# Pooled attention, then a gated MLP: joining a pair's two sums on one set of partitions, a first load on another queue, and a new order

## The chip, the cores and the metric

The kernel runs on one core of a Trainium2 chip. The metric is the device time of one execution in microseconds. The profile is one execution recorded by the hardware profiler; its span is the time from the first to the last instruction, and the execution's own time is a little longer. PE is TensorE, PEld its weight loads, DVE VectorE, ACT ScalarE, POOL GpSimd, SP SyncE, whose queue issues nearly all DMAs; SPq is that issuing.

## The reference

```python
def _attn_ref(q, k, v):                       # q, k, v: (4, 8, 1152, 64) float32
    q_pool = q.reshape(B, H, S // 2, 2, D).mean(axis=3)
    scores = scale * np.matmul(q_pool, k.transpose(0, 1, 3, 2))
    scores = scores - np.max(scores, axis=-1, keepdims=True)
    attn = np.exp(scores)
    attn = attn / (np.sum(attn, axis=-1, keepdims=True) + 1e-09)
    return np.matmul(attn, v)

def _moe_ref(x, w_in, w_out):                 # w_in: (512, 2048), w_out: (2048, 512), float64
    h = x @ w_in
    g = h * np.clip(h + 3.0, 0.0, 6.0) / 6.0
    return g @ w_out

x = attn_out.transpose(0, 2, 1, 3).reshape(B * S // 2, H * D)     # (2304, 512)
return _moe_ref(x, w_in, w_out)
```

## The kernel before

The attention runs over 16 pairs g of heads (4 batches, 4 pairs of two heads j), each with 576 pooled queries in two halves h of 288 (HQ); a unit is one pair and one half. Keys are 9 tiles t of 128. For each unit, scores with the keys on the partitions go to PSUM (line 406 in the first four pairs, the early ones, with plain float32 matmuls for both heads in one tile; line 410 in the late pairs, with operands split into a high and a low part); ScalarE copies them to the tile `s` (step "cp") and VectorE keeps a running maximum (step "mx", line 428). `fold`, `best` and `spread` (steps "s1" to "s3") turn the maxima, reduce them and spread them back over the partitions; `lessen` (step "su", line 449) subtracts, `expo` exponentiates on ScalarE, `values` multiplies with v (line 474).

The denominators come in three ways. In the early pairs `sums_of_four` (line 499) adds up on TensorE, and `pick_sums` (line 510) turns the sums so that queries are on the partitions. In the late pairs GpSimd adds the nine exponentiated tiles of one head to one (`total`, line 467, four steps "ad"). In pairs 4 to 9 `sums` (line 491) multiplies those tiles by a column of ones, six matmuls for a unit; VectorE takes the reciprocal of the small result (`recip`), `widen` repeats it 64 times, `quotient` (line 546) turns it back and `divide` multiplies. From pair 10 on (`BROAD`) `wide_sums` (line 524) multiplies them by 64 columns of ones, so that a sum stands on each of 64 partitions; `take_sums` adds the epsilon on ScalarE, `invert` takes three reciprocals of 128 x 96 on VectorE (line 532), `times` multiplies. `split_x` splits the result in two parts, and `spill` writes both to DRAM.

The MLP weights are float64 and are converted on the chip: `load_raw` loads half a block (lines 572 and 577, one buffer for each half), `convert` takes seven steps "cv" over ScalarE, GpSimd and VectorE (lines 592 to 616; steps 2 to 4 hold a PSUM slot), and `save_w` writes the result to DRAM. There are 16 blocks f of two halves. The first ten (FCV) use one of the three PSUM slots "v", which the early scores use too. When they and the early maxima are done, the step "second" closes these pools and opens those of the late pairs and of the MLP.

Six chunks of 256 tokens of the MLP run mixed with the late pairs: `do_layer` (line 187), relu, gate, split, `do_project` (line 220), 16 steps each. The last 768 tokens come after the attention in a loop of their own, whose last results `store` scales and `write` writes in pieces of at most 96 rows.

The order is made by a planner at build time (class `Order`). Each step has a place, a cost for each engine on which it may run (a third number is added to its place for that engine), the steps that it needs, and the rooms that it takes and frees. Whenever an engine is free, the ready step with the lowest place goes next; if nothing of a lower place is ready, a later one does. The result is each engine's order, which holds on the chip. The constants at the top (FIRST, STEPS, LAG for the MLP, CONV and CSTEP for the conversion, PER for a pair, AT for the parts of a pair) make the places. `load_k`, `load_q`, `load_v` and all other loads are issued by SP in this order.

Of the kernel before, what the change touches and what calls it, by code (L numbers as in the profile page):

```python
# [11 lines left out]
F32 = mybir.dt.float32  # L12
# [9 lines left out]
FIRST, STEPS, LAG = 91.73, (6.01, 2.86), 10.18  # L22
CONV, CSTEP = 9.8, 8.97
# [3 lines left out]
OFF = ((1, 2), (2,))  # L27
BROAD = 10
ADDS = (2, 4, 0)
CUT = 200  # L30
PER, AT, NGL = 25.1, (-3.2, 3.43, -1.21, 3.22, 4.48, 22.08, 16.57), 10.01
TAIL = 768


def adds(g, h):
    return ADDS[0] if g < ADDS[2] else ADDS[1]


# [92 lines left out]
def pooled_attention_then_gated_mlp(ctx, tc, q, k, v, w_in, w_out, out):  # L131
# [96 lines left out]
    def write(ob, c0):  # L228
        r = 0
        while r < P:  # L230
            blk, p0 = divmod(c0 + r, QP)
            n = min(QP - p0, P - r)
            b, tt = divmod(blk, QT)
            nc.sync.dma_start(out=ov[b, tt, p0:p0 + n, :], in_=ob[r:r + n, :])
            r += n

    def store(pool, po, c0):
        for t, o in enumerate(po):
            ob = pool.tile([P, DM], F32, tag="ob", name="ob", bufs=len(po))
            scale(ob, o, "DVE" if t % 2 else "ACT")  # L240
            write(ob, c0 + t * P)
# [18 lines left out]
    with ExitStack() as a:  # L260
# [14 lines left out]
        ones = const.tile([P, D], F32, name="ones")  # L275
        nc.vector.memset(ones, 1.0)
        pick = const.tile([P, 2], F32, name="pick")
# [3 lines left out]
        eps = const.tile([P, 1], F32, name="eps")  # L281
        nc.vector.memset(eps, EPS)
# [146 lines left out]

        def fold(eng, u):  # L430
# [89 lines left out]

        def wide_sums(eng, g, h):
            ps = d_t["p", g, h] = ps_m["s"].tile([P, HQ], F32, tag="s", name="psr")
            for j in range(2):
                nc.tensor.matmul(ps[j * D:(j + 1) * D, :], ones, d_t.pop((g, h, j))[:, 0], start=True, stop=True)  # L524

        def take_sums(eng, g, h):
            x_t[g, h] = xo.tile([P, HQ], F32, tag="x", name="x")
            nc.scalar.activation(out=x_t[g, h], in_=d_t.pop(("p", g, h)), func=AF.Identity, bias=eps)

        def invert(eng, g, h, n):  # L530
            x = x_t[g, h][:, n * QP:(n + 1) * QP]
            nc.vector.reciprocal(out=x, in_=x)

        def times(eng, g, h):
            x = x_t[g, h]
            nc.vector.tensor_tensor(out=x, in0=av_t.pop((g, h)), in1=x, op=ALU.mult)
# [129 lines left out]
        room = dict(kr=1, qr=1, qp=1, vr=2, kT=2, v=3, q=2, mb=2, s=3, S=SBUFS, m=2, st=1, d=2, av=1, x=2, xo=2,  # L666
# [4 lines left out]
        UNIT = PER / 4  # L671

        for g in range(NG):
            lead = PER * (g - 1)
            early = g == 0
            add(("lk", g), lead - 8, {"SP": (940, 3500, 1800)}, partial(load_k, g=g), (), ("kr",))
            add(("lq", g), lead - 7, {"SP": (470, 2500, 1800)}, partial(load_q, g=g), (), ("qr",))
            z = lead + AT[0]
# [223 lines left out]
```

## Time and profile before

| | us |
|---|---|
| median of 3 runs (lowest, highest) | 921.22 (919.14, 922.02) |
| the profiled execution | 917.72 |
| its span, first to last instruction | 915.9 |
| TensorE busy in the span | 871.7 |
| mean granted TensorE clock, share of full speed | 0.983 |

A row of a group of instructions names the line, the engine and operation, the tile written and the tile read, the shapes and the count; then busy time, mean duration of one in ns, and idle time of the engine ahead of them with what ended it. One float32 matmul may show as several records. Busy time is the union of the records, whose ends are modelled for TensorE.

### The profile page before, as it was taken

To read this page: it belongs to the slowest core of one execution; us is meant where nothing else is said; L and a number is where in the kernel's file an instruction comes from. 1 tells how busy PE (TensorE), PEld (TensorE's weight loads), DVE (VectorE), ACT (ScalarE), POOL (GpSimd) and SP (SyncE) were. 2 spreads that over 40 slices of the span, in tenths; PEclk is the share of its full clock that TensorE was granted. 3 is DMA by queue.
4 is the path that set the end of the run, shared out by engine and by line. 5 is a ranking of instruction groups with operands and counts; after the bars stand their busy time and mean duration, and the time that the engine had idled before them with its cause. 6 is when DMAs were issued, how large, how long until landed. Compare 5 with 4: busy or idle time off the path is not lost.

```text
span 915.9 us, 16896 instructions
## 1 busy us (share of the span) xinstructions
PE 871.7 (95%) x5988; PEld 683.8 (75%) x5988; DVE 639.2 (70%) x1196; ACT 585.3 (64%) x1239; POOL 527.4 (58%) x460
## 2 busy tenths in 40 slices
PE   5689997899999999999999999999999999999997
PEld 3344544467787788888988788888888877888886
DVE  2887888887978888867877777777868754322222
ACT  3677978767877767767777676776757753322222
POOL 1666887476977866768667584848576666000000
PEclk9798999899999999999999999999999999999999
DMA  8688665689976485888757787897857749533323
GB/s 218 199 270 261 209 226 200 201 269 355 300 248 186 152 247 184 255 256 254 267 177 245 220 271 228 279 290 251 266 179 249 249 162 315 187 120 138 133 98 92
DMA packets 113395, 203.99 MB, mean 223 GB/s; under 512 B 44448, under 2 KB 68000, under 8 KB 113312
## 3 DMA queue, kind: packets, MB, share of 16 engines
q1 hardware_dynamic: 113312, 202.93, 68.1%
q8 instruction: 47, 0.77, 0.3%
q14 instruction: 36, 0.29, 0.1%
HBM read 171.97 MB, written 30.93 MB: 222 GB/s over the span
## 4 chain that ended last, share of the span: by engine, by line
PE 78%; DVE 8%; ACT 5%; DMA 5%; issue 3%; SPq 0%; POOL 0%; DVEq 0%; ACTq 0%
PE ph L187 21%; PE po L220 16%; PE pav L474 14%; PE pqk L410 12%; PE pt L220 5%; DVE m L428 3%; DMA raw<-in_moe_w_in_dram 2%; PE pst L434 2%; ACT s L312 2%; PE pst L444 2%; ACT s L457 1%; PE pt L384 1%; DVE kT L369 1%; PE pv L406 1%; DMA raw<-in_moe_w_out_dram 1%
## 5 line engine op out<-in xcount | busy, mean ns | idle before, releaser
L457 ACT ACTIVATE s<-s 128x864 f32<-128x864 f32 x192 | 176.9, 930 | 24.6 <-DVE s L449 19.7
L312 ACT COPY s<-pqk 128x288 f32<-128x288 f32 x432 | 158.8, 400 | 48.3 <-PE pqk L410 45.7
L449 DVE TENSOR_TENSOR s<-s,pst 128x864 f32<-128x864 f32 x168 | 174.6, 1044 | 17.8 <-PE pst L444 15.0
L187 PE MATMUL ph<-mxmxh,w 128*128 128x256 f32 x896 | 181.0, 285 | 0.0
L428 DVE TENSOR_TENSOR m<-pqk,m 128x288 f32<-128x288 f32 x336 | 150.6, 448 | 29.0 <-ACT s L312 20.2
L474 PE MATMUL pav<-s,vr 128*64 128x288 f32 x1152 | 158.0, 420 | 2.0 <-DVE x L550 2.0
L187 PEld LDWEIGHTS ph<-mxmxh,w 128*128 128x128 f32 x896 | 146.6, 190 | 3.6 <-issue 1.8
L192 ACT ACTIVATE r<-ph,three 128x256 f32<-128x256 f32 (+1 forms) x128 | 64.2, 501 | 130.3 <-PE ph L187 124.6
L410 PE MATMUL pqk<-qh,kT 128*128 128x288 f32 x432 | 135.7, 327 | 3.9 <-DVE m L428 3.3
L220 PE MATMUL po<-w,gh 128*128 128x512 f32 x448 | 139.3, 392 | 0.0
L467 POOL TENSOR_TENSOR d<-s 128x864 f32<-128x864 f32 x48 | 99.1, 2072 | 62.2 <-PE psr L524 32.0
L196 DVE SCALAR_TENSOR_TENSOR r<-r,ph 128x256 f32<-128x256 f32 (+1 forms) x128 | 57.3, 448 | 100.2 <-ACT r L192 99.6
L205 POOL TENSOR_TENSOR gl<-r,gh 128x256 fp32r<-128x256 f32 x96 | 71.0, 740 | 97.6 <-ACT gh L200 95.3
L187 PE MATMUL ph<-mxmxl,w 128*128 128x256 f32 x448 | 126.5, 282 | 0.0
L474 PEld LDWEIGHTS pav<-s,vr 128*64 128x64 f32 x1152 | 78.6, 140 | 61.5 <-issue 11.4
L410 PE MATMUL pqk<-ql,kT 128*128 128x288 f32 x432 | 121.7, 294 | 0.0
L467 POOL TENSOR_TENSOR d<-d,s 128x864 f32<-128x864 f32 x48 | 98.4, 2058 | 0.2
L410 PEld LDWEIGHTS pqk<-qh,kT 128*128 128x128 f32 x432 | 81.3, 188 | 21.6 <-DVE m L428 7.5
L220 PEld LDWEIGHTS po<-w,gh 128*128 128x128 f32 x448 | 84.3, 188 | 14.6
L220 PE MATMUL po<-w,gl 128*128 128x512 f32 x224 | 90.2, 402 | 1.0 <-DMA w<-w_d 1.0
L187 PEld LDWEIGHTS ph<-mxmxl,w 128*128 128x128 f32 x448 | 85.3, 190 | 0.8
L410 PEld LDWEIGHTS pqk<-ql,kT 128*128 128x128 f32 x432 | 81.8, 189 | 1.9
(94 smaller groups left out, 1409.3 us busy)
## 6 DMA issues: line engine op xcount, KB each, us to landing
w<-w_d SPq DMA_DIRECT2D x224, 512.0 KB, 4.9
w_d<-scratch SPq DMA_DIRECT2D x32, 512.0 KB, 4.5
kr<-in_k_dram SPq DMA_DIRECT2D x32, 288.0 KB, 4.5
qr<-in_q_dram SPq DMA_DIRECT2D x16, 576.0 KB, 6.1
vr<-in_v_dram SPq DMA_DIRECT2D x16, 576.0 KB, 5.3
raw<-in_moe_w_in_dram SPq DMA_DIRECT2D x16, 512.0 KB, 4.8
raw<-in_moe_w_out_dram SPq DMA_DIRECT2D x16, 512.0 KB, 4.3
xh_d<-xh SPq DMA_DIRECT2D x32, 144.0 KB, 5.1
```

The lines of the kernel that those rows point to most:

```text
L187: nc.tensor.matmul(ps, w[:, wi, cs], x[:, c, :], start=(m == 0), stop=(m == 3 * NCC - 1))
L192: nc.scalar.activation(out=r6, in_=ps, func=AF.Relu, bias=three)
L196: nc.vector.scalar_tensor_tensor(out=out, in0=r6, scalar=6.0, in1=ps, op0=ALU.min, op1=ALU.mult)
L205: on.tensor_tensor(out=gl, in0=r6, in1=gh.bitcast(F32), op=ALU.subtract)
L220: nc.tensor.matmul(o, g[:, ts], w[:, wi, :], start=(f == 0 and n == 0), stop=(f == NFC - 1 and n == 2))
L312: nc.scalar.copy(out=out, in_=in_)
L410: nc.tensor.matmul(ps[:, 0:HQ], kT[g][:, j, t, :], w[:, j, :], start=(m == 0), stop=(m == 1))
L428: nc.vector.tensor_tensor(out=m, in0=ps, in1=s0 if t == 1 else m, op=ALU.max)
L449: by[eng].tensor_tensor(out=s, in0=s, in1=m.unsqueeze(1).to_broadcast([P, KC, HQ]), op=ALU.subtract)
L457: nc.scalar.activation(out=s, in_=s, func=AF.Exp, scale=SCALE)
L467: by[eng].tensor_tensor(out=out, in0=x, in1=y, op=ALU.add)
L474: nc.tensor.matmul(av_t[g, h][j * D:(j + 1) * D, :], vr_t[g][:, j, t, :], s_t[g, h][:, j, t, :], start=(t == 0), stop=(t == KT - 1),)
```

## The change

It has five parts.

- In all late pairs the sums of a unit's two heads are brought onto one set of partitions. `total` leaves for each head one tile of 128 x 288. `cross_d` copies the half of it that stands on the other head's partitions across on ScalarE, and `join_d` adds it on GpSimd to the half that is in place, so that one tile holds head 0's sums on partitions 0 to 63 and head 1's on 64 to 127. `sums` then turns this tile in three matmuls against two columns (`side`). `recip`, `widen`, `quotient` and `divide` follow in all late pairs; `wide_sums`, `take_sums`, `invert` and `times` are gone. The buffer of `total` is freed by `join_d`.
- The first q load is issued by ScalarE's queue in place of SP's.
- The first two weight loads no longer need the third score tile of the first unit, but the first q load.
- In the last `store`, the second piece of each tile is written by ScalarE's queue.
- The planner's numbers are new: the MLP steps have a place and a slope for each chunk, the early and late pairs have lengths and offsets of their own, the first conversion blocks stand 61.91 apart instead of 8.97 (a pair is 18.78 long instead of 25.1). The subtractions of the early pairs and the last conversion step may now run on either of two engines.

```diff
-FIRST, STEPS, LAG = 91.73, (6.01, 2.86), 10.18
-CONV, CSTEP = 9.8, 8.97
+START = (87.43, 132.45, 167.51, 203.63, 242.65, 271.87)
+SLOPE = (2.75, 2.1, 2.22, 2.06, 1.92, 2.98)
+LAG, MLP = 7.02, (-1.15, -3.17, 1.24, -1.49)
+CONV, CSTEP = 2.63, (61.91, 57.95)
-OFF = ((1, 2), (2,))
-BROAD = 10
-PER, AT, NGL = 25.1, (-3.2, 3.43, -1.21, 3.22, 4.48, 22.08, 16.57), 10.01
+BIAS = (-7.49, 43.24, -0.28, -1.15, 4.56, -3.44)
+PER = (18.78, 18.63)
+AT = (-0.5, 4.15, 1.04, 6.8, 12.88, 15.86, 15.32, 25.89, 1.24, 1.83, -0.27, -6.23, -4.87, 10.83)
+ATL = (-0.02, 3.57, -0.63, 7.74, -0.2, 13.46, 14.71, 11.28, -4.83, -1.05, 2.03, 6.28, -10.44, 18.64)
...
-    def write(ob, c0):
+    def write(ob, c0, on=(nc.sync,)):
...
-            nc.sync.dma_start(out=ov[b, tt, p0:p0 + n, :], in_=ob[r:r + n, :])
+            on[r > 0 and len(on) > 1].dma_start(out=ov[b, tt, p0:p0 + n, :], in_=ob[r:r + n, :])
...
-            write(ob, c0 + t * P)
+            write(ob, c0 + t * P, (nc.sync, nc.scalar))
...
+        side = const.tile([P, 2], F32, name="side")
+        nc.vector.memset(side, 0.0)
+        for j in range(2):
+            nc.vector.memset(side[j * D:(j + 1) * D, j:j + 1], 1.0)
...
-            nc.sync.dma_start(out=qr_t[g], in_=q[b, h:h + 2].rearrange("h (p t r) d -> p h t r d", p=QP, r=2))
+            (nc.sync if g else nc.scalar).dma_start(out=qr_t[g], in_=q[b, h:h + 2].rearrange("h (p t r) d -> p h t r d", p=QP, r=2))
...
+        def cross_d(eng, u):
+            g, h, j = u
+            if j == 0:
+                d_t["h", g, h] = dp.tile([P, HQ], F32, tag="dh", name="dh")
+            mine, other = halves(j)
+            copy(eng, d_t["h", g, h][mine], d_t[u][other, 0])
+
+        def join_d(eng, u):
+            g, h, j = u
+            mine, _ = halves(j)
+            x = d_t["h", g, h][mine]
+            by[eng].tensor_tensor(out=x, in0=x, in1=d_t.pop(u)[mine, 0], op=ALU.add)
+
         def sums(eng, g, h):
             d_t["p", g, h] = ps_av.tile([P, 512], F32, tag="av", name="psr")
-            den = d_t["p", g, h][:QP, HQ:HQ + 2 * TQ].rearrange("p (x j) -> p x j", j=2)
-            last = {2: KC, 4: 1}[adds(g, h)]
-            for j in range(2):
-                d = d_t.pop((g, h, j))
-                for x in range(TQ):
-                    for t in range(last):
-                        nc.tensor.matmul(
-                            den[:, x, j:j + 1], d[:, t, x * QP:(x + 1) * QP], ones[:, 0:1], start=(t == 0), stop=(t == last - 1)
-                        )
+            d = d_t.pop(("h", g, h))
+            for x in range(TQ):
+                nc.tensor.matmul(
+                    d_t["p", g, h][:QP, HQ + 2 * x:HQ + 2 * x + 2], d[:, x * QP:(x + 1) * QP], side, start=True, stop=True
+                )
...
-                        add(("su", u, c), z + AT[3] + c, {"DVE": (970, 1045)} if late or c not in OFF[j] else {"POOL": (2000, 2050)}, partial(lessen, u=u, c=c),
+                        add(("su", u, c), z + at[3] + c, {"DVE": (970, 1045)} if late else {"DVE": (970, 1045), "POOL": (2000, 2050, BIAS[0])}, partial(lessen, u=u, c=c),
...
+                    if late:
+                        add(("dx", u), z + at[7], {"ACT": (300, 400)}, partial(cross_d, u=u), [("ad", u, 3)], () if j else ("dh",))
+                        add(("dj", u), z + at[7], {"POOL": (765, 815)}, partial(join_d, u=u), [("dx", u)], (), ("d",))
...
-                 {"POOL": (690, 720), "ACT": (600, 700, 3)}, {"POOL": (1380, 1400)})
+                 {"POOL": (690, 720), "ACT": (600, 700, 3)}, {"POOL": (1280, 1300), "DVE": (640, 720, BIAS[1])})
...
-                z = CONV + CSTEP * (f + h / 2)
+                z = CONV + CSTEP[0] * (min(f, FCV) + h / 2) + CSTEP[1] * max(f - FCV, 0)
...
-                add(("lr", f, h), z - 8, {"SP": (470, 3000, 1550)}, partial(load_raw, f=f, half=h), [("mm", (0, 0, 0), 2)], (f"raw{h}",))
+                add(("lr", f, h), z - 8, {"SP": (470, 3000, 1550)}, partial(load_raw, f=f, half=h), [("mm", (0, 0, 0), 2)] if f else [("lq", 0)], (f"raw{h}",))
...
-            z = FIRST + STEPS[0] * min(m, NFC) + STEPS[1] * max(m - NFC, 0)
+            z = START[c] + SLOPE[c] * f
```

## Rows read from the trace of the kernel before

**Rows 1.** Busy time, share of the span and instructions of each engine, from the page.

```profile
...
PE 871.7 (95%) x5988; PEld 683.8 (75%) x5988; DVE 639.2 (70%) x1196; ACT 585.3 (64%) x1239; POOL 527.4 (58%) x460
```

**Rows 2.** Five stretches: us, busy time (instructions) of each engine, clock, DMA share, GB/s.

```profile
...
0.00:156.00 156.00, 127.74 (x916) 69.78 (x917) 117.31 (x192) 113.13 (x189) 99.21 (x91) 0.95 0.72 229
156.00:200.00 44.00, 37.67 (x271) 23.28 (x269) 36.57 (x70) 31.00 (x66) 27.06 (x24) 0.88 0.69 223
200.00:330.00 130.00, 126.99 (x918) 104.17 (x918) 108.98 (x216) 97.89 (x224) 98.68 (x87) 1.00 0.75 248
330.00:782.00 452.00, 451.97 (x3255) 378.51 (x3252) 339.98 (x656) 307.87 (x699) 302.46 (x260) 1.00 0.75 243
782.00:916.00 134.00, 127.35 (x639) 108.04 (x637) 36.36 (x65) 35.36 (x64) 0.00 (x0) 0.99 0.36 122
```

**Rows 3.** The first 20 us, same view and columns.

```profile
...
0.00:20.00 20.00, 10.29 (x44) 7.07 (x44) 3.13 (x14) 6.82 (x11) 2.64 (x8) 1.00 0.80 204
```

**Rows 4.** Instructions in order of time, 0 to 40 us: start, us, engine, line.

```profile
...
0.73 1.28 ACT L312 ACT_TABLE_LOAD   x1 [0.73 <-PEq L887]
...
0.74 1.48 SPq L296 DMA_DIRECT2D kr<-in_k_dram  x2
...
2.26 1.20 SPq L301 DMA_DIRECT2D qr<-in_q_dram  x1
...
6.08 2.15 PE L350 MATMUL pv<-ident,kr 128*128 128x128 f32 x9 [6.08 <-DMA kr<-in_k_dram]
...
9.85 1.02 DVE L322 TENSOR_TENSOR qp<-qr 96x384 f32<-96x384 f32 x2 [7.69 <-DMA qr<-in_q_dram]
...
12.88 1.33 PE L406 MATMUL pv<-qh,kT 64*128 64x288 f32 x4 [0.73 <-ACT qh L312]
...
17.73 1.28 SPq L572 DMA_DIRECT2D raw<-in_moe_w_in_dram  x1
```

**Rows 5.** The chain that ended last, to 60 us: start, us, what.

```profile
...
45.11 6.82 DMA raw<-in_moe_w_in_dram
```

**Rows 6.** Instructions on the raw weight tile, to 160 us: min/median/max ns, first and last start.

```profile
...
L592 ACT ACTIVATE scratch<-raw x22: 658/682/715, 23.0 to 155.7; 128x512 f32<-128x512 f32 x22
...
L609 DVE SCALAR_TENSOR_TENSOR scratch<-raw,pv x20: 643/675/689, 28.6 to 150.5; 128x512 uint32<-128x512 uint32 x20
L572 SPq DMA_DIRECT2D raw<-in_moe_w_in_dram x11: 372/383/1806, 17.7 to 145.3; - x11
...
L605 DVE SCALAR_TENSOR_TENSOR pcv<-raw,pcv x1: 697/697/697, 157.0 to 157.0; 128x512 uint32<-128x512 uint32 x1
...
DMA to landing us min/median/max: 3.4/4.6/6.8
```

**Rows 7.** TensorE's groups of instructions between 300 and 780 us.

```profile
...
L491 PE MATMUL psr<-ones,d 128*96 128x1 f32 x96 | 8.8, 218 | 0.0
L524 PE MATMUL psr<-d,ones 128*64 128x288 f32 x48 | 8.3, 425 | 0.0
L546 PE MATMUL psr<-ident,rw 96*128 96x96 f32 x27 | 3.8, 248 | 0.0
```

**Rows 8.** Groups of instructions of the whole run, shapes kept apart.

```profile
...
L467 POOL TENSOR_TENSOR d<-d 128x288 f32<-128x288 f32 x96 | 77.8, 812 | 0.7
...
L532 DVE RECIPROCAL x<-x 128x96 f32<-128x96 f32 x36 | 26.3, 739 | 7.0 <-ACT x L528 6.9
...
L312 ACT COPY x<-pav 128x288 f32<-128x288 f32 x13 | 5.2, 400 | 10.2 <-PE pav L474 10.1
L510 PE MATMUL psr<-pick,sc 128*96 128x2 f32 x48 | 5.1, 222 | 0.4 <-ACT sc L312 0.4
```

**Rows 9.** Instructions in order of time at the end: VectorE's last, SP's last two.

```profile
...
910.35 0.69 DVE L224 TENSOR_SCALAR ob<-pt 128x512 f32<-128x512 f32 x1 [0.67 <-PE pt L220]
...
912.02 1.00 SPq L234 DMA_DIRECT2D out_dram<-ob  x2
```

More of the change, by code (lines that the diff above doesn't have):

```diff
@@ L519, in recip @@
             nc.vector.reciprocal(out=den, in_=den)
[L521 to L536, printed above, removed]
         def widen(eng, g, h):
@@ L689, in pooled_attention_then_gated_mlp @@
                 cost = (750, 855) if late else (90 + 92 * n, 190 + 92 * n)
-                add(("kh", g, c), z + 2 + c, {"ACT": cost} if late else {"ACT": cost, "DVE": (68 + 133 * n, 150 + 133 * n, .5)},
+                add(("kh", g, c), z + 2 + c, {"ACT": cost} if late else {"ACT": cost, "DVE": (68 + 133 * n, 150 + 133 * n, BIAS[2])},
                     partial(keep_k, g=g, c=c),
@@ L729, in pooled_attention_then_gated_mlp @@
                     z = z0 + (UNIT if late or j else 2 * UNIT)
-                    add(("s1", u), z + AT[2], {"PE": (330, 550)}, partial(fold, u=u), last, ("st",), ("m",) if j else ())
-                    add(("s2", u), z + AT[2], {"DVE": (474, 550)}, partial(best, u=u), [("s1", u)])
-                    add(("s3", u), z + AT[2], {"PE": (250, 470)}, partial(spread, u=u), [("s2", u)])
+                    add(("s1", u), z + at[2], {"PE": (330, 550)}, partial(fold, u=u), last, ("st",), ("m",) if j else ())
@@ L737, in pooled_attention_then_gated_mlp @@
                             [("s3", u) if late else ("sb", u)] + ([("su", u, c - 1)] if c and late else []), (),
                             (("st",) if c == 2 else ()) if late else (("st", u, 3), ("mb", u, 3)))
-                        add(("ex", u, c), z + AT[3] + 1 + c, {"ACT": (831, 930)}, partial(expo, u=u, c=c), [("su", u, c)])
-                    na = 4 if late else adds(g, h)
-                    for n in range(na if late else 0):
+                        add(("ex", u, c), z + at[3] + 1 + c, {"ACT": (831, 930)}, partial(expo, u=u, c=c), [("su", u, c)])
@@ L742, in pooled_attention_then_gated_mlp @@
+                    for n in range(4 if late else 0):
                         cost = 2000 if n < 2 else 765
-                        add(("ad", u, n), z + AT[4] + 1.5 * n, {"POOL": (cost, cost + 50)}, partial(total, u=u, n=n),
+                        add(("ad", u, n), z + at[4] + 1.5 * n, {"POOL": (cost, cost + 50)}, partial(total, u=u, n=n),
                             [("ex", u, c) for c in (range(2) if n == 0 else (2,) if n == 1 else ())] + ([("ad", u, n - 1)] if n else []),
                             () if n else ("d",), (("S", u[:2], 3),) if n == 1 else ())
-                y = z + AT[5]
@@ new lines, in pooled_attention_then_gated_mlp @@
+                if late:
+                    add(("de", g, h), z, {"PE": (510, 730)}, partial(sums, g=g, h=h),
+                        [("dj", (g, h, j)) for j in range(2)] + [("av", g, h, n)], ("av",), ("dh",))
+                else:
+                    add(("o4", g, h), ya, {"PE": (2700, 2900)}, partial(sums_of_four, g=g, h=h), [("av", g, h, n)], ("av",), ("S",))
+                    add(("sc", g, h), ya, {"ACT": (300, 400)}, partial(keep_sums, g=g, h=h), [("o4", g, h)])
+                    add(("de", g, h), ya, {"PE": (510, 730)}, partial(pick_sums, g=g, h=h), [("sc", g, h)])
```

88 lines of the change are left out of this document (38 added, 50 removed).

## The prediction

> **What bounds the kernel now.** I read the page's busy shares first: TensorE is busy for 95% of the span and VectorE, the next, for 70% [rows 1]. A share over the whole span hides where the missing 5% lies, so the next view is the busy time cut into five stretches [rows 2]. TensorE stands idle for 156.00 - 127.74 = 28.3 us before 156 us, 6.3 us from 156 to 200, 3.0 us from 200 to 330, nothing (0.03 us) from 330 to 782, and 6.7 us from there to the end: 44.3 us in all. In the 452 us of the long middle stretch the engine is never without work, at a granted clock of 1.00 (the 2.4 GHz level). Nothing that relieves VectorE, ScalarE or GpSimd there can shorten the run, only TensorE work that goes away. The time to be won by a new order lies almost wholly before 200 us: 34.6 us of idle TensorE, plus what the lower clock level costs (mean granted clock 0.95 and 0.88 in the two stretches, a mixture of the 1.2 and 2.4 GHz levels, the lower after moments in which the engine waited).
>
> Then the start in order of time [rows 4]: k is issued at 0.74 us, TensorE begins at 6.08 us, the first q is issued at 2.26 us behind both k loads and ends the wait of VectorE only at 9.85 us, and the first scores begin at 12.88 us. The first weight load is issued at 17.73 us. Last the chain of waits before 60 us [rows 5] and the rows of the raw weight tile [rows 6]: the chain runs through weight loads (one stands in it for 6.82 us), and eleven loads of the first half of a block are issued between 17.7 and 145.3 us, one per 12.8 us. The pools of the second half of the program can be opened only when ten blocks (20 halves) are converted, and the last early conversion ends at about 151 us; the first conversion step in the new pools begins at 157.0 us [rows 6], so the opening lies a little before. So the conversion loop is one of the two things that can set the end of the early part; the other is the attention of the four early pairs, whose TensorE work fills 127.7 us of the 156.
>
> **The change part by part.** First q by ScalarE's queue: ScalarE has only a table load before the first turned k, so the issue costs nothing there [rows 4]. The q issue can move from 2.26 us to 0.73 us or, behind the 1.28 us table load, to 2.0 us: 0.3 to 1.5 us earlier. q then competes with k, which now lands alone by 6.08 us; if k lands later, the nine k turns (2.15 us) move later too; they end at 8.2 us and q comes at 9.85, so k has 1.6 us to spare. Bounds: 0 and 2 us won; I take 1.0, nearer the middle of the issue's move. The DMA share is 0.80 in the first 20 us [rows 3], so the transfers are already close. The Trainium skill speaks against this step: its page "DMA: Bandwidth & Descriptors", section "Issuing engines are not separate DMA queues", says that transfers issued by several engines run on the same 16 DMA engines and interleave, and that only the sequencer's issue time is saved. No row here shows two issuing engines side by side; by that rule the term would be 0 to 1.2 us (the issue of q lasts 1.20 us), and the sum about 1 us smaller.
>
> First weight loads: they hung on the third score block and go out at 17.73 us; now they hang on the q load alone, in a queue that is empty from about 4 to 8 us. That is some 14 us earlier, and with 12.8 us per block it is about one whole turn of the loop. The cost of putting 1.0 MB more in front of the k of pair 1 is covered: pair 1's scores come behind all 18 score blocks of pair 0.
>
> Order of the early part: the conversions are spread evenly now (8.97 per block); in the new list the first half block stands at 2.63, the next at 33.6, then 64.5, 126 and so on up to 560, while the four early pairs end at 75. So from the fourth half on they fill gaps. VectorE has the gaps: 117.3 us busy of 156, of which the 60 conversion steps are 41 us (20 x 3 x 0.675) [rows 2, 6]. If they fall into gaps, the scores no longer queue behind them, and the early part is bounded by TensorE's own 127.7 us. The two bounds of this term are all of the idle time from 20 to 156 us, 28.3 - 9.7 = 18.6 us [rows 2, 3], and nothing. I take half, 9.3 us: the conversion loop, started 14 us earlier, no longer forbids it, but the chains score, copy, maximum through three PSUM slots stay.
>
> The subtractions of the early pairs may go to VectorE or GpSimd, and the last conversion step to VectorE far behind its place; both engines have over a quarter of the time free before 200 us. Zero of its own; its gain is in the half above. If that cover went, it would show as lost idle time within the same two bounds.
>
> Denominators, pairs 4 to 9: twelve one-column matmul records per unit (a unit is one pair and one query half; 144 records, 96 of them after 300 us at 8.8 us, so 1.1 us per unit) become six two-column ones of the kind that the early pairs have, 5.1 us for 8 units, 0.64 [rows 7, 8]. Twelve units: -5.5 us of TensorE. Pairs 10 to 15: the two wide sums (8.3 us for 12 units, 0.69) become six such records (0.64) and three turns of the quotient (0.42: 3.8 us for 27) [rows 7, 8]: +0.37 x 12 = +4.4 us. TensorE sum: -1.1 us, all in the stretch where it is the bound. Bounds -3 and +1, by the spread of the rows.
>
> Added: 48 copies of 64 x 288 across halves on ScalarE, by the 400 ns row of the 128 x 288 copy 19 us; 48 additions on GpSimd at 812 ns, 39 us [rows 8]; removed: 36 reciprocals of 739 ns on VectorE, 26.6 us [rows 8]. ScalarE is busy for 308 and GpSimd for 302 of the 452 us [rows 2], so both have room; the change moves them by 4 and 8% of that stretch. The half copy waits for the last of four GpSimd additions, and behind it on ScalarE stand exponentials and score copies; GpSimd's own additions wait for no TensorE step any more, since the buffer is freed by the addition of the halves. Cost 0 while TensorE always has MLP work queued; without that cover, 48 waits of some 0.5 us, 24 us at worst. I take 0, because the present bundle of waits in that stretch costs TensorE 0.03 us.
>
> End: the last tile's pieces are issued one behind the other by SP, the last two from 912.02 to 913.02 us, after VectorE finishes at 911.04 [rows 9]. With the second piece on ScalarE's queue, 0.4 to 1.0 us is won; I take 0.7. The new places of the MLP steps: TensorE has no gap to fill after 330 us, so 0.
>
> Sum: -1.0 - 9.3 - 1.1 - 0.7 = -12.1 us. The profiled execution has a span of 915.9 and a time of 917.7 us, so its like would be 905.6; the median of the three runs shown is 921.2, 3.5 us above that execution, and I put the sum against the median: 909.
>
> **The rivals.** *Starved conversions (slower).* With blocks at places 126 to 560 everything else goes first, and the opening of the second half waits for the twentieth half block while TensorE runs dry. A block that is still to be done then costs its load, 4.6 us, a ScalarE step of 0.68, a GpSimd step that I put at the same, and three VectorE steps, 2.0: about 8 us [rows 6], with the two halves side by side. From two blocks late on it costs more than the rest wins: 2 x 8 + a second clock drop of some 3 us, less 2.8 us of the other terms and what little the attention gained, gives about +10 us, 931. For it: the places; against it: VectorE's gaps, 39 us before 156 us, nearly as much as all the conversion steps need.
>
> *Nothing left (same).* The early part ends earlier, but what bounds it is TensorE plus the chain through three PSUM slots, of which a filling conversion holds one while its steps wait for gaps; the 9.3 us then shrink to about 1. With the other terms that is 918 to 922. A variant gives the same time: the copies on ScalarE wait for GpSimd where MLP work runs short.
>
> *More.* All 18.6 us are won, and TensorE stays at its higher clock from 156 to 200 us, worth 44 x 0.12 = 5 us: -26, 895. For it: the opening of the second half is an empty spot that a better order fills; against it: no order so far in this trace keeps TensorE full before 200 us.
>
> **How the numbers follow.** Forecast (some 5 to 18 us won) 0.54, more 0.12, same 0.12, starved or otherwise slower 0.22. A measurement of this kernel can tell about 0.3%, 2.8 us, from no change. Faster 0.66, same 0.12, slower 0.22. The range goes from the lower end of the sum with all idle time won (895) to a starved loop by one and a half blocks (925), which leaves out some 2 in 10.
>
> **What would show it.** Right: first scores ahead of 12 us; raw loads issued before 8 us; the first k turn into the second half's pool at 140 to 150 us in place of 156; TensorE idle before 200 us down to about 24 us; still no idle time from 330 to 780 us; three sum matmuls per unit; the run's last issue 0.5 to 1 us after VectorE's last scale. What would make it wrong: a stretch before the opening in which TensorE is idle and VectorE runs only conversion steps; TensorE waits on denominators or on ScalarE behind a half copy after 330 us; or MLP work that runs short and leaves TensorE with gaps in the middle.

## The result, and the profile after

The changed kernel takes 912.13 us (median of 4 runs, 908.85 to 913.61) against 921.06 us for the kernel before on the same chip (4 runs, 919.14 to 922.02): a ratio of 0.9895 over the single runs, interval 0.987 to 0.992 (the two medians alone give 0.990). The forecast was 909 us in a range of 895 to 925. The sign and nearly the size came out, -8.9 us for a forecast of -12.1. The place of the gain did not, as the first view shows. The profiled execution took 911.55 us with a span of 909.4.

Busy time in the stretches of [rows 2], with the same columns, the fourth one only up to 760 us (the tail of the MLP starts earlier now), kernel after:

```profile
0.00:156.00 156.00, 129.29 (x908) 70.35 (x910) 129.04 (x207) 112.09 (x187) 84.76 (x80) 0.92 0.75 226
156.00:200.00 44.00, 38.18 (x303) 25.61 (x296) 38.43 (x73) 33.04 (x71) 28.55 (x24) 0.92 0.76 234
200.00:330.00 130.00, 128.43 (x919) 105.19 (x918) 115.57 (x225) 102.78 (x238) 105.05 (x95) 1.00 0.83 267
...
330.00:760.00 430.00, 429.01 (x3137) 363.77 (x3136) 314.99 (x628) 315.65 (x724) 331.36 (x299) 1.00 0.75 240
```

TensorE's idle time fell from 28.3 to 26.7 us before 156 us, from 6.3 to 5.8 up to 200, from 3.0 to 1.6 up to 330, and it is 1.0 us from 330 to 760: 35.1 us over these stretches against 37.6. That is 2.5 us, and the spans of the two profiled executions lie 6.5 us apart (915.9 and 909.4; the medians 8.9). So idle time doesn't tell the whole. Busy time isn't a fixed price of the work either. The kernel before needs 871.7 us of it [rows 1]; one of the experiments below (e2) runs the same TensorE instructions in another order and shows 885.6. Its granted clock was 0.974 over a span of 936.4 us, against 0.983 over 915.9: 24.1 and 15.3 us of full speed missing, so about 9 of the 14 us can be the clock. Where records end is modelled, so that a short wait inside a row of matmuls may also count as busy; how much of the rest that is, no row shows.

So I counted the work done as well. The table takes the TensorE instructions that all kernels here share (turns, scores, folds, values, the sums of the early pairs, the MLP), each record at the duration that it has where records follow each other densely (0.126 us for a record of the values, 0.14 for late scores, 0.119 and 0.23 for the MLP's two layers), summed up to a time. Which durations the small groups are given moves an entry by up to 1.6 us, so smaller differences say little. The first column is before's sum in us, the others are by how many us another kernel is ahead of it:

```
t us  before | after    e1    e2    e3    e4    e5    e6    e7    e8    e9   e10   e11   e12
  80    53.6 |  -1.5  -2.4  -3.1  -4.6  +2.3  -1.4  +0.7  +1.5  -2.2  -1.8  -0.8  -2.6  +2.3
 156   122.0 |  -1.2  -3.1  -4.3  -8.0  -0.6  -2.3  -0.5  -1.2  -2.1  -0.8  -3.9  -4.2  +0.7
 200   150.8 |  +2.0  -1.8  -2.6  -5.1  -0.9  -1.6  +0.5  +2.5  +1.7  +2.6  -3.8  -3.2  +6.2
 250   198.2 |  +2.0  -1.8  -5.3  -6.7  +1.2  -2.0  -0.1  +3.4  +2.2  +3.3  -7.5  -6.7  +6.1
 330   272.8 |  +6.6  -0.7  -3.8  -5.9  -1.1  -7.1  +0.1  +5.7  +0.4  +7.8  -7.8  -6.0 +11.3
 500   441.9 |  +9.1  -1.5  -4.4  -8.6  -0.6  -9.4  -0.3  +8.4  +1.8 +10.7  -6.8  -9.3 +14.0
 700   646.4 |  +8.4  -2.2 -16.4  -8.9  -1.4 -14.5  -0.3  +6.9  +1.6  +5.8 -11.6 -10.1 +14.0
```

The kernel after is 1.2 us *behind* at 156 us, gains 7.8 us between 156 and 330 us, and keeps what it has from there on. Of these 7.8 us, 1.9 are idle time (0.5 + 1.4). The granted clock from 156 to 200 us rose from 0.88 to 0.92 (a mixture of the levels of 1.2 and 2.4 GHz), some 1.8 us of 44. The matmuls of the denominators that the table leaves out take 2.6 us less: from 156 to 200 us 2.7 us before and 2.8 after, from 200 to 330 us 8.0 and 5.3. That makes 6.3 of the 7.8, and what remains, 1.5 us, is no more than the table's own uncertainty. Before 156 us it is the other way round: 1.6 us less idle time, but a granted clock of 0.92 in place of 0.95.

What changed at the border of the two stretches shows in TensorE's instructions in order of time. Kernel before (the first turns of k into the new pools start at 155.63 us):

```profile
155.63 0.82 PE L350 MATMUL pt<-ident,kr 128*128 128x128 f32 x6
...
162.94 3.15 PE L474 MATMUL pav<-s,vr 128*64 128x288 f32 x12
...
171.95 0.40 PE L410 MATMUL pqk<-qh,kT 128*128 128x288 f32 x1
```

Kernel after, same view:

```profile
156.78 0.88 PE L348 MATMUL pt<-ident,kr 128*128 128x128 f32 x6
...
163.87 0.59 PE L408 MATMUL pqk<-qh,kT 128*128 128x288 f32 x1
...
165.11 2.37 PE L475 MATMUL pav<-s,vr 128*64 128x288 f32 x12
```

Both kernels open the second half's pools at nearly the same time, but before's TensorE does three groups of values first, the first of them in 3.15 us (the same group takes 1.68 us at the higher clock level), and the late scores begin 16.3 us after the first turn. In after they begin 7.1 us after it and the values lie between them. Late scores are what VectorE's work hangs on, and VectorE has more of it from then on: 38.4 us of 44 and 115.6 of 130 against 36.6 and 109.0 [rows 2]. Early late scores are not enough by themselves, though: in e2 and e8 below they begin 7.1 us behind the first turn as well, in e3, e4 and e11 8.4 to 9.3 us, and by the table these five gain between -1.8 and +2.5 us from 156 to 330 us.

The start, instructions in order of time as in [rows 4], kernel after:

```profile
0.73 0.41 ACTq L299 DMA_DIRECT2D qr<-in_q_dram  x1
0.73 1.47 SPq L294 DMA_DIRECT2D kr<-in_k_dram  x2
...
5.51 0.47 SPq L565 DMA_DIRECT2D raw<-in_moe_w_in_dram  x1
5.74 1.02 DVE L320 TENSOR_TENSOR qp<-qr 96x384 f32<-96x384 f32 x2 [3.39 <-DMA qr<-in_q_dram]
...
8.21 2.15 PE L348 MATMUL pv<-ident,kr 128*128 128x128 f32 x9 [8.21 <-DMA kr<-in_k_dram]
...
12.05 0.98 PEld L404 LDWEIGHTS pv<-qh,kT 64*128 64x128 f32 x6 [1.02 <-ACT qh L310]
```

q comes 4.1 us earlier and k 2.1 us later; the first scores start at 12.05 us (12.88 before).

The raw weight tile up to 160 us as in [rows 6], kernel after:

```profile
L602 DVE SCALAR_TENSOR_TENSOR scratch<-raw,pv x20: 665/678/690, 17.0 to 153.6; 128x512 uint32<-128x512 uint32 x20
L565 SPq DMA_DIRECT2D raw<-in_moe_w_in_dram x12: 373/383/472, 5.5 to 157.8; - x12
```

The loop starts 12.2 us earlier (load at 5.5, not 17.7; first of these steps at 17.0, not 28.6) and ends 3.1 us *later* (153.6, not 150.5).

The sums of the late pairs, TensorE's groups from 300 to 780 us as in [rows 7], kernel after:

```profile
L501 PE MATMUL psr<-side,dh 128*96 128x2 f32 x120 | 11.8, 214 | 0.0
L539 PE MATMUL psr<-ident,rw 96*128 96x96 f32 x60 | 8.2, 245 | 0.0
```

And the end as in [rows 9], kernel after:

```profile
903.57 1.93 ACTq L230 DMA_DIRECT2D out_dram<-ob  x3
904.19 0.69 DVE L220 TENSOR_SCALAR ob<-pt 128x512 f32<-128x512 f32 x1 [0.67 <-PE pt L216]
```

VectorE ends at 904.88 us and the last issue 0.62 us behind it (903.57 + 1.93); before it was 1.98 us.

### The profile page after: what moved, and what is told of

Read it like the earlier page. It is cut to its first block, busy times and chain, and to the rows that moved or that the text cites. A ratio compares the mean times of both kernels' runs of the same rounds, so it can differ in the third digit from the quotient of the medians.

```text
span 909.4 us, 17050 instructions
## 1 busy us (share of the span) xinstructions
PE 866.5 (95%) x5976; PEld 685.1 (75%) x5976; DVE 637.9 (70%) x1202; ACT 603.5 (66%) x1292; POOL 552.0 (61%) x499
## 4 chain that ended last, share of the span: by engine, by line
PE 75%; DVE 8%; DMA 6%; ACT 5%; issue 3%; POOL 1%; SPq 1%; DVEq 0%; ACTq 0%
PE ph L183 20%; PE po L216 15%; PE pav L475 13%; PE pqk L408 12%; PE pt L216 5%; DVE m L426 3%; DMA raw<-in_moe_w_out_dram 2%; PE pst L435 2%; PE pst L445 2%; ACT s L310 2%; DMA w<-w_d 1%; PE pt L382 1%; DVE s L450 1%; PE pv L404 1%; PE pt L348 1%
## 5 line engine op out<-in xcount | busy, mean ns | idle before, releaser
L310 ACT COPY s<-pqk 128x288 f32<-128x288 f32 x432 | 160.2, 400 | 28.6 <-PE pqk L408 25.8
L475 PEld LDWEIGHTS pav<-s,vr 128*64 128x64 f32 x1152 | 78.9, 139 | 59.8 <-issue 13.2
L201 POOL TENSOR_TENSOR gl<-r,gh 128x256 fp32r<-128x256 f32 x96 | 72.4, 754 | 25.8 <-ACT gh L196 18.6
```

Of the source, the lines that this page charges most:

```text
L201: on.tensor_tensor(out=gl, in0=r6, in1=gh.bitcast(F32), op=ALU.subtract)
L310: nc.scalar.copy(out=out, in_=in_)
L475: nc.tensor.matmul(av_t[g, h][j * D:(j + 1) * D, :], vr_t[g][:, j, t, :], s_t[g, h][:, j, t, :], start=(t == 0), stop=(t == KT - 1),)
```

## Experiments

A part can be tried in two ways. Edited in the kernel's source, it makes the planner draw up a new list, and then hundreds of about 2,840 of TensorE's rows stand in another place (e1 to e4; 891 in e1). Or the list of one kernel is written out and issued again as it stands, with only the part exchanged (e5 to e7, e12). e8 to e11 change one planner number by an amount without meaning, to see what another list costs by itself. All kernels compute everything.

### The denominators alone (e1, e5)

e1 puts the new steps into the kernel before; the planner makes a new list:

```diff
-BROAD = 10
+BROAD = 100
...
+                    if late:
+                        add(("dx", u), z + AT[4] + 5, {"ACT": (300, 400)}, partial(cross_d, u=u), [("ad", u, 3)], () if j else ("dh",))
+                        add(("dj", u), z + AT[4] + 5, {"POOL": (765, 815)}, partial(join_d, u=u), [("dx", u)], (), ("d",))
...
-                        add(("de", g, h), z, {"PE": (cost, cost + 220)}, partial(sums, g=g, h=h),
+                        add(("de", g, h), z, {"PE": (510, 730)}, partial(sums, g=g, h=h),
```

> The kernel before with the new denominators alone: half copies on ScalarE, joining on GpSimd, three sum matmuls in all late pairs, wide sums gone; planner numbers, loads and stores as before. Theory A (the denominators only trade TensorE work, 30.5 us of sum and quotient records before against 28.2 after): 919 us, 0.995 to 1.000 of before, and TensorE still without idle time from 330 to 780 us. Rival B (GpSimd's 43 us of waits for the sum matmuls are what held the late pairs back, and freeing the buffer early brings the gain of the whole change): 912 to 914 us, 0.99.

Measured: 925.89 us, ratio 1.0055 [1.0028, 1.0082]; neither theory. In the table it falls behind by 3.1 us before 156 us, where no late denominator exists yet, so its loss is at least partly its list's.

e5 therefore keeps before's list. Every step stands where it stood, only the denominators' steps are exchanged, the small ones directly behind the sums (92 of TensorE's rows differ).

> The new denominators alone, as in e1, but with the list of before kept: the planner's old list is replayed step by step on the same engines, and only the denominator steps are exchanged and the half copies put in (92 of some 2,840 rows of TensorE's order differ, against 891 in e1). Theory A (e1 lost 0.5% because its list fell out worse, not through the denominators): 917 to 921 us, 0.996 to 1.001. Rival B (the half copies and the longer chain cost time by themselves): 923 to 927, like e1.

Measured: 937.76 us, 1.0192 [1.0166, 1.0218], the slowest of all and beyond both theories. It loses from 250 us on, wherever there are late denominators. TensorE's instructions on the tile of the sums from 200 to 760 us, what they waited for and who waited for them, in e5:

```profile
its engine sat idle before it (us, times) until:
  ACT rw L317: 3.1, 7
  ACT x L317: 2.7, 5
  POOL dh L502: 1.4, 1
...
who waited for it (us, times):
  DVE den L533: 13.3, 6
```

The same part of the view for the kernel after, same window:

```profile
its engine sat idle before it (us, times) until:
who waited for it (us, times):
  DVE x L543: 1.1, 2
  DVE den L526: 0.4, 1
```

In e5 VectorE stands 13.3 us waiting for the sums, and TensorE waits 7.2 us in turn for copies and for a joined half. In after the same chain causes no wait of TensorE at all and 0.4 us of VectorE's small step. The new chain is longer (addition, half copy, joining, sums, reciprocal, widening, turning), and it is free only where its steps are spread out in the list. What e5 prices is the new chain at this one place; a better place in before's list wasn't tried.

### The order alone (e2)

The kernel after with the denominators of before:

```diff
-            d = d_t.pop(("h", g, h))
-            for x in range(TQ):
-                nc.tensor.matmul(
-                    d_t["p", g, h][:QP, HQ + 2 * x:HQ + 2 * x + 2], d[:, x * QP:(x + 1) * QP], side, start=True, stop=True
-                )
+            den = d_t["p", g, h][:QP, HQ:HQ + 2 * TQ].rearrange("p (x j) -> p x j", j=2)
+            last = 1
+            for j in range(2):
+                d = d_t.pop((g, h, j))
+                for x in range(TQ):
...
+        def wide_sums(eng, g, h):
```

> The changed kernel with the denominators of before (six one-column matmuls in pairs 4 to 9, wide sums from pair 10 on), all else as changed: new places, early loads, first q on ScalarE's queue, last store on two queues. Theory A (order and start bring 6 to 7 of the 8.9 us): 914 to 915 us, 0.993. Rival B (the denominators bring it): 920 us, 0.998 to 1.000.

Measured: 929.62 us, 1.0114 [1.0053, 1.0175]. The new places without the new denominators are slower than the kernel before, and both theories fall. The profiled execution was the slowest of the four, 938.38 us (the others 928.06 to 930.24). GpSimd's groups from 330 to 760 us, in e2:

```profile
L472 POOL TENSOR_TENSOR d<-s 128x864 f32<-128x864 f32 x33 | 67.3, 2061 | 44.7 <-PE psr L496 27.9 <-PE psr L529 15.6 <-ACT s L462 0.9
```

GpSimd's additions wait 43.5 us for TensorE's sums (27.9 + 15.6), since the buffer of `total` comes free only there, and TensorE is idle for 6.1 us of this stretch. In after `join_d` frees that buffer. But these waits don't explain the loss: the kernel before has the same ones, 42.1 us, while its TensorE is idle for 0.03 us. GpSimd's waits in the same stretch, in the kernel before:

```profile
POOL d L467 <- PE psr L524: 32.0, 10, 5.6
POOL d L467 <- PE psr L491: 10.1, 6, 2.9
```

Of the 6.1 us in e2 only 1.5 end with GpSimd's additions. Each half of the change loses when the planner makes a list for it alone. That order and denominators were fitted to each other would explain it, but these runs don't show it: the two losses, 0.55 and 1.14%, are no larger than what a new list costs by itself (e8 to e11).

### The start (e3, e6, e12)

e3: the one dependency of the first loads, in the kernel before, list drawn up anew.

```diff
-                add(("lr", f, h), z - 8, {"SP": (470, 3000, 1550)}, partial(load_raw, f=f, half=h), [("mm", (0, 0, 0), 2)], (f"raw{h}",))
+                add(("lr", f, h), z - 8, {"SP": (470, 3000, 1550)}, partial(load_raw, f=f, half=h), [("mm", (0, 0, 0), 2)] if f else [("lq", 0)], (f"raw{h}",))
```

> The kernel before with one edit: the first two weight loads need the first q load in place of the third score tile. Theory A (the conversion loop sets the end of the early part, at one block per 12.8 us): the first conversion step in the new pools comes about 10 us earlier than 157 us and the time falls by 6 to 10 us, 912 to 915. Rival B (VectorE and the chain of scores through three PSUM slots set that end, the loop only fills): the opening stays within 3 us of 157 and the time within 3 us of before.

Measured: 922.98 us, 1.003 [1.0005, 1.0055]. It is 8.0 us behind at 156 us, and the first turn of k into the new pools comes at 163.2 us. Theory A falls, and so does the opening that rival B named (within 3 us of 157). Earlier loads alone win nothing here, in that list.

e6: before's list as it stands, with the first q on ScalarE's queue and the first two raw loads behind the first v.

```diff
-            nc.sync.dma_start(out=qr_t[g], in_=q[b, h:h + 2].rearrange("h (p t r) d -> p h t r d", p=QP, r=2))
+            (nc.sync if g else nc.scalar).dma_start(out=qr_t[g], in_=q[b, h:h + 2].rearrange("h (p t r) d -> p h t r d", p=QP, r=2))
...
+        first = [("lr", 0, 0), ("lr", 0, 1)]
...
```

> The kernel before with its own list, on which only the start is changed: the first q is issued by ScalarE's queue and the first two weight loads move up in SP's queue to right behind the first v. All other engines keep their order exactly. Theory A (an earlier start helps little, since the steps that use it stand where they stood; only the first scores come earlier): first scores at about 12 us in place of 12.88, time 0 to 2 us less than before, 0.998 to 1.000. Rival B (the conversion loop sets the end of the early part): 6 to 10 us less, 0.99.

Measured: 918.31 us, 0.9975 [0.9951, 1.0000]: -2.7 us for the two start edits together, with an interval that just reaches no change. First scores at 11.11 us. Rival B (6 to 10 us less) falls.

e12: after's list as it stands, the first q back on SP.

```diff
-            (nc.sync if g else nc.scalar).dma_start(out=qr_t[g], in_=q[b, h:h + 2].rearrange("h (p t r) d -> p h t r d", p=QP, r=2))
+            nc.sync.dma_start(out=qr_t[g], in_=q[b, h:h + 2].rearrange("h (p t r) d -> p h t r d", p=QP, r=2))
```

> The changed kernel with its own list and one DMA back: the first q is issued by SP behind both k loads. TensorE, VectorE and GpSimd keep their order. Theory A (the second queue only saves the time of the issue, and q and k share the same transfers: with it q lands at 5.7 and k at 8.2 us, without it k at about 6 and q at about 10): first scores at 12.5 to 13 us in place of 12.05, time 0 to 1 us more, 912 to 913. Rival B (q came earlier at no cost to k, so that undoing it costs the whole 2 us): first scores at 14 us, 914.

Measured: 907.42 us, 0.9864 [0.9826, 0.9901]; the lowest time of all, and faster than the kernel before. Its interval overlaps that of after, so the two aren't told apart, but a gain of the second queue is not to be seen. The start, in order of time, in e12:

```profile
2.25 1.31 SPq L299 DMA_DIRECT2D qr<-in_q_dram  x1
...
5.80 2.15 PE L348 MATMUL pv<-ident,kr 128*128 128x128 f32 x9 [5.80 <-DMA kr<-in_k_dram]
...
8.12 1.02 DVE L320 TENSOR_TENSOR qp<-qr 96x384 f32<-96x384 f32 x2 [5.77 <-DMA qr<-in_q_dram]
...
11.15 1.95 PEld L404 LDWEIGHTS pv<-qh,kT 64*128 64x128 f32 x10 [1.02 <-ACT qh L310]
```

With one queue k lands first (5.80 us, not 8.21) and q behind it (8.12, not 5.74), and here the first scores start 0.9 us earlier than with two. The scores need both. Over all profiles the seven kernels with one queue have k at 5.4 to 6.8 us, q at 8.1 to 10.4 us (with the same issue times) and the first scores at 11.15 to 13.38, mean 12.24; the seven with two have k at 7.3 to 8.6, q at 5.5 to 6.0 and the scores at 11.11 to 12.36, mean 11.98. That is 0.26 us on average, in a scatter of 2 us: q gains what k loses. The two groups differ in more than the queue: all seven with two queues also issue a weight load at 5.4 to 5.8 us, and of those with one queue only e3 and e12 issue theirs before the first scores. So the average isn't the price of the queue alone; e12 against after is the one pair that differs in nothing else. The rule that the prediction cites from the Trainium skill ("DMA: Bandwidth & Descriptors", "Issuing engines are not separate DMA queues") agrees, and its lower bound of 0 was nearer than my 1.0.

### The conversion's last step (e4, e7)

VectorE is busy for 129.0 us before 156 us, not 117.3 as before; 18 of the 32 last conversion steps run on it now. My second theory was that this work ate the gain of the early part.

e4, list drawn up anew:

```diff
-                 {"POOL": (690, 720), "ACT": (600, 700, 3)}, {"POOL": (1280, 1300), "DVE": (640, 720, BIAS[1])})
+                 {"POOL": (690, 720), "ACT": (600, 700, 3)}, {"POOL": (1280, 1300)})
```

> The changed kernel with the last conversion step on GpSimd alone, as before. Theory A (VectorE is the bound of the early part, 129 of 156 us busy against 117 before, because 11 of the 20 last steps moved to it at 0.96 us each, and this ate what the earlier loads gave): VectorE's busy time before 156 us falls by about 10 us, the opening of the second half comes 5 to 10 us earlier than 156 us and the time falls to 903 to 908. Rival B (conversions that stand behind everything else are what delays the opening): opening and time within 3 us of the changed kernel's 156 and 912. Rival C (GpSimd becomes the bound): 915 to 920.

Measured: 920.87 us, 1.001 [0.9985, 1.0035], nearest to rival C, but in a new list. e7 does the same in after's list as it stands:

```diff
+        plan = [(k, f, "POOL" if k[0] == "cv" and k[3] == 6 else e, t) for k, f, e, t in od.run()]
```

> The changed kernel with its own list, in which the last conversion steps that stood on VectorE (18 of 32) run on GpSimd at the same place; TensorE, ScalarE and SP keep their order exactly. Theory A (those steps are a load on VectorE, the bound of the early part, and e4 lost through its list): 907 to 911 us. Rival B (the list needs them on VectorE, since GpSimd takes 1.28 us in place of 0.8 and stands in the way of its subtractions): 914 to 920.

Measured: 910.86 us, 0.9896 [0.9873, 0.992], the time of after. That lies at the upper end of theory A's range and can't be told from no change. Its first stretch:

```profile
0.00:156.00 156.00, 130.63 (x913) 71.28 (x913) 121.74 (x198) 111.94 (x187) 96.66 (x91) 0.91 0.75 228
```

VectorE is relieved of 7.3 us there, TensorE is idle for 25.4 us in place of 26.7, the granted clock is 0.91 in place of 0.92, and the first turn into the new pools comes at 156.0 us. So these steps on VectorE are not what kept the early part from ending sooner. What e4 lost beyond e7 came with its new list.

### What another list costs by itself (e8 to e11)

```diff
-PER = (18.78, 18.63)
+PER = (18.80, 18.65)
```

(e8, in after; e9, in after: `LAG` 7.02 to 7.3; e10, in before: `PER` 25.1 to 25.13; e11, in before: `CONV` 9.8 to 10.1.)

> The changed kernel with a change that means nothing: the length of a pair in the planner is 18.80 and 18.65 in place of 18.78 and 18.63. The planner's list falls out otherwise (810 rows of TensorE's order differ). Theory A (the gain belongs to this one list, found among many, not to a part of the change): 917 to 923 us, the gain gone. Rival B (the gain comes from the parts and the coarse placing): within 3 us of the changed kernel, 909 to 915.

> The changed kernel with another change that means nothing: the lag of the second MLP product in the planner is 7.3 in place of 7.02 (628 rows of TensorE's order differ). Theory A (about half of the gain belongs to the one list, the rest to the parts, as e8 with 0.9955 showed): 914 to 919 us, 0.993 to 0.998. Rival B (e8 was an unlucky list): 909 to 913, 0.990. Rival C (all of the gain belongs to the list): 920 or more.

> The kernel before with a change that means nothing: the length of a pair in the planner is 25.13 in place of 25.1 (827 rows of TensorE's order differ). Theory A (the list of before is a chosen one as well, so that any other costs about 5 us): 923 to 928 us, 1.003 to 1.008. Rival B (the list of before is an ordinary one): within 3 us of 920.

> The kernel before with its conversion blocks placed 0.3 later in the planner (10.1 in place of 9.8; 619 rows of TensorE's order differ). Theory A as for e10: 923 to 928 us. Rival B: within 3 us of 920.

Measured, as ratios to the kernel before: e8 0.9955 [0.9927, 0.9982] (916.38 us), e9 0.9924 [0.9905, 0.9943] (914.41), e10 1.0114 [1.0092, 1.0137] (931.79), e11 1.006 [1.0043, 1.0077] (927.05). e8 lies between its two theories, e9 and e11 came out as theory A said, e10 above it. A nudge without meaning costs after 0.3 to 0.6% and before 0.6 to 1.1%: both kernels hold lists that are better than the two neighbours tried of each (for e9 that is not certain, since its interval overlaps that of after). Two things follow. An experiment on one part through the planner carries 0.3 to 1.1% that the part didn't cause, as large as what e1, e3 and e4 were to measure. And the change is more than one lucky list: the mean of the two nudged versions of after is 0.994 and that of before 1.0087, a ratio of 0.985, which is an estimate from two lists on each side.

What one such list costs can be seen in e8. From 200 to 330 us TensorE is idle for 5.3 us there (1.6 in after), and 4.5 of them are one wait for VectorE's running maximum. VectorE stood until then on a single last step of the conversion, a subtraction that takes 0.69 us where nothing disturbs it. The stretch, and instructions in order of time, in e8:

```profile
200.00:330.00 130.00, 124.74 (x869) 102.27 (x869) 111.79 (x210) 97.60 (x223) 99.56 (x92) 0.97 0.79 259
...
246.88 5.95 DVE L609 TENSOR_TENSOR scratch<-scratch 128x512 fp32r<-128x512 f32 x1
247.28 2.07 POOL L468 TENSOR_TENSOR d<-d,s 128x864 f32<-128x864 f32 x1
...
251.47 0.80 POOL L468 TENSOR_TENSOR d<-d 128x288 f32<-128x288 f32 x1
252.75 1.01 DVE L426 TENSOR_TENSOR m<-pqk,m 128x288 f32<-128x288 f32 x2
253.81 0.88 PE L435 MATMUL pst<-ident,m 128*96 128x128 f32 x3 [4.49 <-DVE m L426]
```

GpSimd had begun an operation 0.30 us before the subtraction and ran five more without a gap; the subtraction ended 0.56 us behind the last of them (252.27 and 252.83). After the wait TensorE's granted clock was at the lower level for a while (a record of the late scores takes 0.44 us at 254.72 us and 0.29 before the wait): 0.97 over this stretch, against 1.00 in after, some 3.5 us of 130. Wait and clock together cover the 5.9 us that e8 gains less than after from 200 to 330 us. This is one profiled execution, but it shows how a nudge can cost half a per cent: it lets one step of VectorE meet a row of GpSimd operations.

## Why the prediction came out as it did

*Early part, -9.3 us: wrong in its place.* I took half of TensorE's 18.6 idle microseconds from 20 to 156 us. What was to show it didn't come: the first turn of k in the new pools is at 156.78 us and not at 140 to 150, the idle time before 200 us is 32.5 us (26.7 + 5.8) and not about 24, and the work done by 156 us is 1.2 us less. The step that failed is "the conversion loop, started 14 us earlier, no longer forbids it". The loop did start 12.2 us earlier, but it took 13.8 us between loads ((157.8 - 5.5) / 11) in place of 12.8, and its last early step came later than before. e3 and e7 show that neither earlier loads nor a lighter VectorE opens the pools sooner by itself. What does bound the opening I can't name from these runs; e12, which differs from after in one queue, opened at 152.2 us. The rows point to the other side of my sentence, the chains of score, copy and maximum: from 20 to 156 us, 10.0 us of TensorE's waits in after end with VectorE's running maximum (6.4 before), the longest with this one:

```profile
36.11 0.76 PE L404 MATMUL pv<-qh,kT 64*128 64x288 f32 x4 [2.10 <-DVE m L426]
```

And the 1.6 us of idle time that were won before 156 us went to the lower granted clock (0.92 for 0.95, some 3 us).

*What stood in its place:* +7.8 us of work between 156 and 330 us, a stretch in which I had put at most 5 us, in the rival "more", and for the clock. By the rows it is 2.6 us of removed denominators, 1.9 of idle time and 1.8 of clock. The order that goes with it has the late scores 7.1 in place of 16.3 us behind the first turn and a VectorE that is fuller in the whole stretch; that this order is the cause is argued and not shown, since e2, e4 and e8 have the early late scores too and gain at most 2.5 us. e9 and e12, which share most of this order, gain 8.6 and 10.6 us there, and the kernels with before's places (e1, e3, e5, e6, e10, e11) -4.8 to +2.4. Which of the new place numbers does it stays open. In e8 a nudge of 0.02 loses it from 200 us on (-1.3 us from 200 to 330), by the one long subtraction shown above. The prediction gave that subtraction's move to VectorE "zero of its own"; e7 shows that this held in after's list, and e8 that it need not in the next.

*"The time to be won lies almost wholly before 200 us":* this came from idle time alone. From 156 to 330 us there were 9.3 us of it; 1.9 were won, and 7.8 us of work with it, since the clock and the denominators came on top.

*Start, -1.0 us:* the first scores came 0.83 us earlier in this pair of profiles, at 12.05 and not ahead of 12, but 0.26 us on average over all of them. The failed step is "k has 1.6 us to spare": k came 2.1 us later. The raw loads were issued at 5.51 us, as forecast. Both start edits on a list held fixed gave -2.7 us, interval -4.5 to 0 (e6). The second queue by itself isn't seen to win anything (e12).

*Denominators:* TensorE's records for sums and quotients went from 30.5 us (13.2 + 8.3 + 9.0, whole run) to 28.2 (14.2 + 14.0), -2.3 us for -1.1, inside the bounds of -3 and +1. The two halves came in the order forecast: from 200 to 500 us 18.7 became 12.3 us (-6.4 for -5.5), from 500 to 800 us 8.3 became 12.0 (+3.7 for +4.4). The half copy took 431 ns (forecast 400) and the joining 800 (812). "Cost 0 while TensorE always has MLP work queued" held in after (no wait of TensorE on those tiles from 200 to 760 us, 1.0 us of idle time from 330 to 760; the 2.5 us from there to 782 end with weight loads, 1.6 us, and with ScalarE's step of the gate, 0.9) and not in e5, which has the MLP work of before's list: 16.7 us, near the 24 us given as the worst. Each engine's order is fixed, so MLP work that stands behind the sums can't be done while they wait. The cover that I named, queued MLP work, is thus not sufficient.

*End, -0.7 us:* the span's end less the end of VectorE's last scale is 5.17 us on average in the seven kernels that end with one queue (4.89 to 5.43) and 4.54 in the seven with two (4.28 to 5.09): -0.63 us.

*The rivals:* "starved conversions" didn't happen (the opening kept its time; its own sum, 2 x 8 + 3 - 2.8, gives +16 and not the +10 written there), and half of "nothing left" did: the early part gave nothing, as it said. That the time still fell was due to a stretch which the forecast had left at nothing. So the size is right in part by chance: a term of -9.3 us that was not there was made up for by one of some 8 us in another place, of which I had listed only the denominators.

## What to carry to other kernels

Where an order has changed, add up the bounding engine's work done by a given time and compare it between the two traces; idle time misses the granted clock and work that went away, and here it missed most of the gain. Try a part in an order that is held fixed, and nudge the planner once or twice without meaning to learn what any new list costs (0.3 to 1.1% here) before a difference of that size is put down to the part. A longer chain that relieves the bounding engine is free only if its steps are spread over the list: the same chain cost 1.9% at one place, and caused no wait of TensorE at others. Before a step with two SBUF inputs moves to VectorE, look at what GpSimd runs at that time.

## What the runs showed of the hardware

A subtraction of two SBUF tiles on VectorE took 675 to 2458 ns for one shape (median 806, 18 of them in after), and 5947 ns in the case of e8 shown above. It is long where GpSimd has begun an operation just ahead of it. VectorE and GpSimd in order of time in after, the longest case there:

```profile
244.82 2.46 DVE L609 TENSOR_TENSOR scratch<-scratch 128x512 fp32r<-128x512 f32 x1
...
```

```profile
244.68 2.04 POOL L468 TENSOR_TENSOR d<-d,s 128x864 f32<-128x864 f32 x1
246.67 1.18 POOL L201 TENSOR_TENSOR gl<-r,gh 128x256 fp32r<-128x256 f32 x1
```

And a case with nothing on GpSimd beside it:

```profile
98.55 0.69 DVE L609 TENSOR_TENSOR scratch<-scratch 128x512 fp32r<-128x512 f32 x1 [0.21 <-ACT scratch L310]
```

GpSimd's addition ends at 246.72 us; with the 0.69 us of the free case behind it that makes 247.41, and the subtraction ends at 247.28. GpSimd's next step takes 1.18 us (mean of that step 0.75), as if it had waited for VectorE in turn. The Trainium skill says so in "SBUF — State Buffer", section "SBUF: two separate sides": an operation of VectorE with two SBUF inputs and a GpSimd operation that reads SBUF exclude each other, and the one that comes second is blocked for the whole of the other. These rows agree. The case of e8 goes further: there VectorE was held through six GpSimd operations in a row, 5.39 us, and not through one. In the first 156 us of after it is small: eleven such steps average 958 ns, 270 more than the free case, about 3 us of VectorE's time. One of them, 2.29 us at 33.09 us, stands right ahead of the 2.10 us wait of TensorE shown above; still e7, which has none of them on VectorE, takes no less time.

The mean granted clock of the first 156 us fell from 0.95 to 0.92 in after, and over all the kernels here it lies between 0.91 and 0.96 for nearly the same work. In before, TensorE waited 1.62, 0.64, 0.45 and 0.53 us in the 7 us ahead of the group of values that took 3.15 us; in after, 0.95, 0.84, 0.76 and 0.50 us in the 7 us ahead of its first one, which took 2.37.

The same q load, issued at the same time in seven one-queue kernels, was there between 8.1 and 10.4 us, and between 8.7 and 9.9 us in the five of them that issue no weight load before the first scores. So a difference of 1 us at the start of one run says nothing of an edit.
